# Local attention in half tiles of 58 queries with 64 keys, and the pooled values of the first batch on GpSimd

## The chip, the core and the metric

The kernel runs on one core of a Trainium2 chip. The metric is the device time of one execution in microseconds (us), the median of several runs. Engines are named as in the profile: PE is TensorE's matmuls, PEld its weight loads, DVE is VectorE, ACT is ScalarE, POOL is GpSimd, SP is SyncE, which here only issues DMAs (SPq). L364 is line 364 of the kernel before, unless a line of the changed kernel is named.

## The reference

Attention over 2 batches, 8 heads, 576 tokens and 64 numbers per head is the sum of two paths. One attends from and to means of 4 tokens (144 positions) and repeats the result; the other attends within fewer than 4 tokens. Its output (1152 tokens by 512) goes through a feed-forward network, then through 8 weighted experts.

```python
q_d, k_d, v_d = means of 4 tokens
out_up = np.repeat(softmax(q_d @ k_d.T / 8) @ v_d, 4, axis=2)
mask = np.abs(pos[:, None] - pos[None, :]) < 4
out_local = softmax(np.where(mask, q @ k.T / 8, -1e9)) @ v
x = (out_up + out_local) as (1152, 512)
h = x @ w_in;  x = softplus(h) @ w_out
P = exp(x @ w_gate), rows and columns normalised 8 times
out = sum over e of P[:, e] * (relu(x @ w1[e]) @ w2[e])
```

## The kernel before

Attention is cut into units. A **pooled** unit (`pooled`, 16 of them) is one batch, one half of the 144 means and two heads; a **local** unit (`local`, 20 of them) is one batch, one tile of 116 queries (5 tiles, the last of 112) and four heads. Both have four steps. In a local unit `s1` puts the mask into a PSUM bank with one bf16 matmul (L356), adds the scores of four heads (L364), takes the negative row maximum on DVE (`nm`, L287) and the exponentials on ACT (`e`, L290). `s2` turns the exponentials on PE (L376) and copies them out on ACT (`ptls`, L378). `s3` multiplies by v (L384; a column of ones gives the sums) and scales on DVE (`ull`, L394). `s4` turns the result (L400), adds the pooled path on DVE (`xf`, L406) and leaves x as a rounded and a remainder part on POOL (L419, L420). All matmuls but the mask's are float32: a plain one takes two passes of TensorE, a transpose one, and the trace counts passes (L364 x8 for four matmuls).

The window of a tile of 116 queries is 122 keys (`KW`), and `vw` holds the v rows of that window, loaded by one DMA a tile into a pool of three buffers.

Around the units stand sums for the pooled path: `pool_qk(b, p)` makes `qd` on DVE (L250) and `ks`, `kd` on POOL (L256, L258), and ACT scales `kd` and `k` (L259, L260); `load_vd(b)` adds four v rows (`vs` L277, `vd` L279), on DVE for the first batch and on POOL for the second.

The first weights of the feed-forward network come as float64; `from_double` (L124 to L137) takes them apart: two ACT steps (`cs`, `cm`), then six on DVE, a copy on ACT and a product on POOL (`w`, L137). `prep(n)` does that for the n-th weight tile. The first products of the network are `ph` (L444) and `py` (L486).

The order is written by hand in `run()`. `order` lists the units, `at` says ahead of which unit an extra piece of work is issued (the second batch's loads at 1 and 9, its `pool_qk` at 11 to 14, `prep` at 16, 19, 23 and 29, pieces of the network from 22 on). `emit` lets the four steps of a unit follow two units apart. A scheduler of the tile framework then sets each engine's final order; an engine takes its instructions strictly in that order. `issue_after(i)` keeps what follows behind the instruction i in that order. At most six PSUM banks serve the units. SP issues nearly all DMAs; a DMA also waits for the landing of the one eight places before it.

Of the kernel before, what the change touches and what calls it, by code (L numbers as in the profile page):

```python
# [21 lines left out]
P = 128  # L22
# [4 lines left out]
KW = QT + 2 * (POOLF - 1)  # L27
NQT = -(-S // QT)
NPAIR = H // 2
DA = D + 1  # L30
CH = 384
# [10 lines left out]
WIN = [min(max(QT * t - POOLF + 1, 0), S - KW) for t in range(NQT)]  # L42
OFF = sorted({QT * t - WIN[t] for t in range(NQT)})
# [33 lines left out]
class Net:  # L77
# [11 lines left out]
    def constants(self):  # L89
# [5 lines left out]
        self.mask = self.atp.tile([P, len(OFF), KW], BF16, tag="mask", name="mask", bufs=1)  # L95
        self.maskf = self.convp.tile([P, len(OFF), KW], F32, tag="cm", name="maskf", bufs=1)
# [109 lines left out]
    def attention_pools(self, stack):  # L206
# [3 lines left out]
        self.vwp = stack.enter_context(tc.tile_pool(name="vwp", bufs=3, side="right"))  # L210
# [51 lines left out]

    def load_vw(self, b, t):
        w = self.vwp.tile([P, H, DA], F32, tag="vw", name=f"vw{b}{t}")
        self.nc.sync.dma_start(out=w, in_=self.a["vw"][b, t].rearrange("p (h d) -> p h d", h=H))
        self.vw[b, t] = w

    def load_vd(self, b):
# [3 lines left out]
        for hf in range(2):  # L272
# [3 lines left out]
            e = nc.vector if b == 0 else nc.gpsimd  # L276
# [6 lines left out]
    def softmax_exp(self, ps, n, m, k, tag):  # L283

        nc = self.nc
        nm = self.atp.tile([m, n], F32, tag="nm" + tag, name="nm")
        nc.vector.tensor_reduce(out=nm, in_=ps, op=ALU.max, axis=AX.X, negate=True)  # L287
        e = self.atp.tile([m, n, k], F32, tag="e" + tag, name="e", bufs=3 if tag == "l" else 2)
        for j in range(n):
            nc.scalar.activation(e[:, j], ps[:, j], AF.Exp, bias=nm[:, j : j + 1])  # L290
        return e
# [55 lines left out]
    def local(self, b, t, g):  # L347
        nc, ident = self.nc, self.ident
        st = {}
        w0 = WIN[t]  # L350
        nq = min(QT, S - QT * t)
        mv = OFF.index(QT * t - w0)

        def s1():
            ps = self.psa.tile([P, 512], F32, tag="a", name="pl")[:nq, : 4 * KW].rearrange("p (j k) -> p j k", j=4)
            nc.tensor.matmul(  # L356
                ps,
                lhsT=self.identb[:nq, :nq],
                rhs=self.mask[:nq, mv : mv + 1, :].to_broadcast([nq, 4, KW]),
                start=True,  # L360
                stop=False,
            )
            for j in range(4):
                nc.tensor.matmul(  # L364
                    ps[:, j],
                    lhsT=self.qT[b, j][:, g, QT * t : QT * t + nq],
                    rhs=self.kT[b, j][:, w0 : w0 + KW],
                    start=False,
                    stop=(j == 3),
                )  # L370
            st["e"] = self.softmax_exp(ps, 4, nq, KW, "l")

        def s2():
            ps = self.psa.tile([P, 512], F32, tag="a", name="ptl")[:KW, : 4 * nq].rearrange("p (j q) -> p j q", j=4)
            for j in range(4):
                nc.tensor.transpose(ps[:, j], st["e"][:, j], ident[:nq, :nq])  # L376
            pt = self.atp.tile([KW, 4, nq], F32, tag="ptl", name="ptls")
# [3 lines left out]
        def s3():  # L381
            ps = self.psa.tile([P, 512], F32, tag="a", name="pvl")[:nq, : 4 * DA].rearrange("p (j d) -> p j d", j=4)
            for j in range(4):
                nc.tensor.matmul(  # L384
                    ps[:, j], lhsT=st["pt"][:, j], rhs=self.vw[b, t][:KW, 4 * g + j], start=True, stop=True
                )
            if g == 1 and NQT * b + t + 3 < B * NQT:
                self.load_vw(*divmod(NQT * b + t + 3, NQT))
            rs = self.atp.tile([nq, 4, 1], F32, tag="rsl", name="rsl")
            nc.vector.tensor_scalar(rs, ps[:, :, D:DA], 1e-9, None, ALU.add)  # L390
            rr = self.atp.tile([nq, 4, 1], F32, tag="rrl", name="rrl")
            nc.vector.reciprocal(rr, rs)
            ul = self.atp.tile([nq, 4, D], F32, tag="ull", name="ull")
            nc.vector.tensor_tensor(ul, ps[:, :, 0:D], rr.to_broadcast([nq, 4, D]), ALU.mult)  # L394
            st["ul"] = ul

        def s4():
            ps = self.psa.tile([P, 512], F32, tag="a", name="pxl")[:, : 2 * nq].rearrange("p (j q) -> p j q", j=2)
            for j in range(2):
                nc.tensor.transpose(  # L400
                    ps[:, j], st["ul"][:, 2 * j : 2 * j + 2].rearrange("p j d -> p (j d)"), ident[:nq, :nq]
                )
# [312 lines left out]
    def run(self):  # L715
# [21 lines left out]
        for t in range(3):  # L737
            self.load_vw(0, t)
# [32 lines left out]

        def prep(n, lag):

            with ExitStack() as st:
                for ins in self.ends[-1 - lag]:
# [165 lines left out]
def arrange(i):  # L941
# [10 lines left out]

    va = np.concatenate([va, np.zeros((B, P - KW, H, DA), f)], 1)
    out["vw"] = np.stack([va[:, w : w + P] for w in WIN], 1).reshape(B, NQT, P, H * DA)
# [3 lines left out]
    r, c = np.arange(QT)[:, None], np.arange(KW)[None]  # L958
    m = [np.where(np.abs(r + o - c) < POOLF, f(0), f(-1e9)) for o in OFF]
    m = np.concatenate([np.stack(m, 1), np.zeros((P - QT, len(OFF), KW), f)], 0)  # L960
    out["mask"] = np.ascontiguousarray(m.astype(f))
# [39 lines left out]
```

## Time and profile before

| | us |
|---|---|
| median of 3 runs | 1067.55 (1067.21 to 1068.75) |
| the profiled execution's own time | 1065.39 |
| its span in the profile | 1063.6 |
| PE busy | 1042.9 (98% of the span) |
| DVE busy | 783.1 (74%) |
| ACT busy | 435.4 (41%) |
| POOL busy | 165.8 (16%) |

The profile is of one execution, 1.8 us longer than its span and 2.2 us under the median. The attention units lie in the first 130 us; from there on PE is busy almost without a gap to the end. So the shares of the whole span tell little of this change, and the views below are cut to the first 130 us. A chain row is a piece of the path that ended last; a timeline row is a run of equal instructions with, in brackets, the idle time ahead of it and what ended that.

### The profile page before, as it was taken

To read this page: it belongs to the slowest core of one execution; us is meant where nothing else is said; L and a number is where in the kernel's file an instruction comes from. 1 tells how busy PE (TensorE), PEld (TensorE's weight loads), DVE (VectorE), ACT (ScalarE), POOL (GpSimd) and SP (SyncE) were. 2 spreads that over 40 slices of the span, in tenths; PEclk is the share of its full clock that TensorE was granted. 3 is DMA by queue.
4 is the path that set the end of the run, shared out by engine and by line. 5 is a ranking of instruction groups with operands and counts; after the bars stand their busy time and mean duration, and the time that the engine had idled before them with its cause. 6 is when DMAs were issued, how large, how long until landed. Compare 5 with 4: busy or idle time off the path is not lost.

```text
span 1063.6 us, 16117 instructions
## 1 busy us (share of the span) xinstructions
PE 1042.9 (98%) x6421; PEld 959.9 (90%) x6421; DVE 783.1 (74%) x1466; ACT 435.4 (41%) x815; POOL 165.8 (16%) x218
## 2 busy tenths in 40 slices
PE   7899999999999999999999999999999999999998
PEld 4789999999998899898989989898998989899896
DVE  6698699999997687784947658484765848576572
ACT  4688687766743433241413324141331414133130
POOL 3463300001112220211202011120201112020000
PEclk9899999999999999999999999999999999999999
DMA  9541032222111221111211111121111112110003
GB/s 250 163 153 62 2 120 79 79 80 80 41 40 40 79 80 40 40 41 39 80 40 40 41 40 41 40 80 40 40 40 40 41 40 79 40 41 1 1 2 89
DMA packets 13035, 63.99 MB, mean 60 GB/s; under 512 B 1760, under 2 KB 2016, under 8 KB 6496
## 3 DMA queue, kind: packets, MB, share of 16 engines
q1 hardware_dynamic: 12320, 61.79, 17.8%
q10 hardware_dynamic: 640, 1.18, 0.4%
q8 instruction: 50, 0.82, 0.3%
q14 instruction: 25, 0.20, 0.1%
HBM read 60.60 MB, written 2.36 MB: 59 GB/s over the span
## 4 chain that ended last, share of the span: by engine, by line
PE 87%; DVE 8%; ACT 2%; DMA 2%; POOL 1%; issue 1%; SPq 0%; DVEq 0%; ACTq 0%
PE po L586 37%; PE pu L537 33%; PE ph L444 7%; PE py L486 6%; PE pl L364 1%; DVE h L465 1%; DMA vr<-in_vp 1%; PE pvl L384 1%; DMA k<-in_k 1%; DVE r L461 1%; DVE l L462 1%; PE pvd L325 1%; DVE l L463 1%; DVE yp L498 0%; PE ptl L376 0%
## 5 line engine op out<-in xcount | busy, mean ns | idle before, releaser
L537 PE MATMUL pu<-T,a 128*128 128x320 f32 (+1 forms) x2688 | 354.2, 293 | 1.4 <-DVE yp L498 1.4
L537 PEld LDWEIGHTS pu<-T,a 128*128 128x128 f32 x2688 | 351.4, 188 | 3.0 <-issue 1.6
L608 DVE SCALAR_TENSOR_TENSOR acc<-po,prob,acc 128x512 f32<-128x512 f32 x126 | 94.1, 749 | 173.5 <-PE po L586 173.5
L586 PE MATMUL po<-w,h 128*128 128x512 f32 x960 | 221.3, 390 | 0.0
L586 PEld LDWEIGHTS po<-w,h 128*128 128x128 f32 x960 | 179.9, 188 | 37.3
L188 ACT CAST w<-raw 128x1024 fp32r<-128x1024 f32 x32 | 33.4, 1052 | 271.4 <-PE po L586 271.4
L586 PE MATMUL po<-w,h0a 128*128 128x512 f32 x576 | 142.3, 390 | 0.6 <-DVE w L189 0.6
L157 POOL TENSOR_TENSOR s<-raw 128x256 f32<-128x256 f32 x32 | 28.5, 891 | 677.6 <-DVE a L168 473.0
L586 PEld LDWEIGHTS po<-w,h0a 128*128 128x128 f32 x576 | 107.3, 188 | 22.5 <-DVE w L189 1.0
L486 PE MATMUL py<-h,w 128*128 128x384 f32 x576 | 104.0, 336 | 1.3 <-DVE h L465 0.8
L444 PE MATMUL ph<-x,w 128*128 128x384 f32 x576 | 104.1, 336 | 0.0
L486 PEld LDWEIGHTS py<-h,w 128*128 128x128 f32 x576 | 99.7, 188 | 2.3 <-DVE h L465 1.3
L444 PEld LDWEIGHTS ph<-x,w 128*128 128x128 f32 x576 | 99.8, 188 | 0.0
L549 ACT ACTIVATE h<-c 128x320 fp32r<-128x320 f32 x128 | 58.6, 468 | 79.8 <-DVE c L560 79.8
L550 DVE SCALAR_TENSOR_TENSOR h<-c,h 128x320 fp32r<-128x320 f32 x128 | 68.1, 540 | 0.3
L560 DVE TENSOR_TENSOR c<-v,pu 128x256 f32<-128x256 f32 (+1 forms) x128 | 57.8, 451 | 11.1 <-PE pu L537 8.2
L549 ACT ACTIVATE h0a<-c 128x256 fp32r<-128x256 f32 x96 | 37.5, 417 | 50.7 <-DVE c L560 50.4
L189 DVE TENSOR_TENSOR w<-raw,w 128x1024 fp32r<-128x1024 f32 x32 | 39.0, 1220 | 22.1 <-ACT w L188 22.1
L586 PE MATMUL po<-w,h0b 128*128 128x512 f32 x192 | 54.2, 389 | 0.0
L586 PEld LDWEIGHTS po<-w,h0b 128*128 128x128 f32 x192 | 36.0, 188 | 7.5
L558 ACT COPY p<-pu 128x256 f32<-128x256 f32 (+1 forms) x64 | 25.1, 392 | 36.1 <-PE pu L537 34.5
L550 DVE SCALAR_TENSOR_TENSOR h0a<-c,h0a 128x256 fp32r<-128x256 f32 x96 | 39.1, 420 | 0.8 <-ACT h0a L549 0.3
(141 smaller groups left out, 1243.2 us busy)
## 6 DMA issues: line engine op xcount, KB each, us to landing
raw<-in_w SPq DMA_DIRECT2D x48, 1024.0 KB, 4.9
vw<-in_vw SPq DMA_DIRECT2D x10, 260.0 KB, 2.9
vr<-in_vp SPq DMA_DIRECT2D x4, 640.0 KB, 8.8
k<-in_k SPq DMA_DIRECT2D x8, 288.0 KB, 6.2
out<-acc SPq DMA_DIRECT2D x5, 256.0 KB, 2.0
q<-in_q SPq DMA_DIRECT2D x8, 144.0 KB, 5.9
out<-acc SPq DMA_DIRECT2D x8, 128.0 KB, 2.3
q0a<-in_q ACTq DMA_DIRECT2D x4, 144.0 KB, 5.6
```

The lines of the kernel that those rows point to most:

```text
L157: nc.gpsimd.tensor_tensor(s[:, 0], a21, a22, ALU.add)
L188: nc.scalar.copy(w[:, 0], raw)
L189: nc.vector.tensor_tensor(w[:, 1], raw, split(w[:, 0]), ALU.subtract)
L444: nc.tensor.matmul(ps[:, i], lhsT=wv[:, a, k, fo : fo + P], rhs=x[:, b, k], start=(n == 0), stop=(n == 3 * KD - 1),)
L486: nc.tensor.matmul(ps[:, a], lhsT=w[:, i, d * P : (d + 1) * P], rhs=h[:, j, f], start=(n == 0), stop=(n == 3 * NFT - 1),)
L537: nc.tensor.matmul(ps, lhsT=w[:, x, a, k], rhs=t[:, y, b, k], start=(m == 0), stop=(m == 5))
L549: act = nc.scalar.activation(hi, src, AF.Relu)
L550: dve = nc.vector.scalar_tensor_tensor(lo, src, 0.0, split(hi), ALU.max, ALU.subtract)
L558: nc.scalar.copy(to, ps)
L560: nc.vector.tensor_tensor(to, src, ps, ALU.add)
L586: nc.tensor.matmul(ps, lhsT=self.h[s, i, f][:, at * P : (at + 1) * P], rhs=w[:, j], start=(n == 0), stop=(n == 3 * NFT - 1),)
L608: nc.vector.scalar_tensor_tensor(acc, ps, pe, acc, ALU.mult, ALU.add)
```

## The change

Each local unit now computes two halves of 58 queries, each as 64 rows against its own window of 64 keys. The two halves of a head lie above each other on 128 partitions: the scores are eight float32 matmuls, each into 64 partitions by 64 columns, and the mask is one matmul of 4 x 64 columns in place of 4 x 122. The exponentials of two heads are then turned together, two transposes of 128x128 in place of four. The product with v takes two heads in one matmul: the v rows of two heads stand on the two halves of the partitions beside blocks of zeros (`places_v`, three fixed buffers, the zeros set once by POOL), four matmuls of 130 columns in place of four of 65. The last turn is a plain matmul with columns of the identity, which drops the 6 rows too many of each half, in place of a transpose; in the last tile it is done in two parts. The v window is loaded by two DMAs of 130 KB in place of one of 260 KB.

The pooled v of the first batch (`vs`, `vd`) moves from DVE to POOL. The second batch's `pool_qk` and the first `prep` are kept behind the last softmax that was issued before them (`self.begun`), and the first `prep` is issued at unit 15 in place of 16.

```diff
-KW = QT + 2 * (POOLF - 1)
+HQ = QT // 2
+KW = HQ + 2 * (POOLF - 1)
...
+    def places_v(self):
+        self.vring = [
+            self.vwp.tile([P, 2, 2, NPAIR, DA], F32, tag=f"vw{i}", name=f"vw{i}", bufs=1) for i in range(VR)
+        ]
+        for w in self.vring:
+            for r in range(2):
+                self.nc.gpsimd.memset(w[(1 - r) * D : (2 - r) * D, :, r], 0.0)
+
     def load_vw(self, b, t):
-        w = self.vwp.tile([P, H, DA], F32, tag="vw", name=f"vw{b}{t}")
-        self.nc.sync.dma_start(out=w, in_=self.a["vw"][b, t].rearrange("p (h d) -> p h d", h=H))
+        w = self.vring[(NQT * b + t) % VR]
+        for r in range(2):
+            self.nc.sync.dma_start(out=w[r * D : (r + 1) * D, :, r], in_=self.a["vw"][b, t, r])
...
-            e = nc.vector if b == 0 else nc.gpsimd
+            e = nc.gpsimd
...
-        nc.vector.tensor_reduce(out=nm, in_=ps, op=ALU.max, axis=AX.X, negate=True)
+        dve = nc.vector.tensor_reduce(out=nm, in_=ps, op=ALU.max, axis=AX.X, negate=True)
...
+        self.begun = (dve.ins, act.ins)
...
-            for j in range(4):
-                nc.tensor.matmul(
-                    ps[:, j],
-                    lhsT=self.qT[b, j][:, g, QT * t : QT * t + nq],
-                    rhs=self.kT[b, j][:, w0 : w0 + KW],
+            for u in range(2):
+                n0, w0 = ROW[2 * t + u], WIN[2 * t + u]
+                for j in range(4):
+                    nc.tensor.matmul(
+                        ps[u * KW : (u + 1) * KW, j],
+                        lhsT=self.qT[b, j][:, g, n0 : n0 + KW],
+                        rhs=self.kT[b, j][:, w0 : w0 + KW],
...
-            for j in range(4):
-                nc.tensor.transpose(ps[:, j], st["e"][:, j], ident[:nq, :nq])
+            for j in range(2):
+                nc.tensor.transpose(ps[:, j], st["e"][:, 2 * j : 2 * j + 2].rearrange("p j k -> p (j k)"), ident)
...
-            for j in range(4):
-                nc.tensor.matmul(
-                    ps[:, j], lhsT=st["pt"][:, j], rhs=self.vw[b, t][:KW, 4 * g + j], start=True, stop=True
-                )
+            for u in range(2):
+                for j in range(2):
+                    nc.tensor.matmul(
+                        ps[u * D : (u + 1) * D, 2 * j : 2 * j + 2],
+                        lhsT=st["pt"][:, j, u * D : (u + 1) * D],
+                        rhs=self.vw[b, t][:, u, :, 2 * g + j],
...
+                if last == KW:
+                    cols = ident.rearrange("p (u q) -> p u q", u=2)[:, :, :HQ]
+                    nc.tensor.matmul(ps[:, j], lhsT=ul, rhs=cols, start=True, stop=True)
+                    continue
+                for o, n, c in ((0, HQ, 0), (HQ, nq - HQ, last)):
+                    nc.tensor.matmul(ps[:, j, o : o + n], lhsT=ul, rhs=ident[:, c : c + n], start=True, stop=True)
...
+        def second(p):
+            with ExitStack() as st:
+                for ins in self.begun:
+                    st.enter_context(self.tc.issue_after(ins))
+                self.pool_qk(1, p)
...
-                for ins in self.ends[-1 - lag]:
+                for ins in self.begun if n == 0 else self.ends[-1 - lag]:
...
-            at.setdefault(11 + p, []).append(lambda p=p: self.pool_qk(1, p))
-        for n, lag, u in zip(range(2 * NFT), (1, 1, 0, 0), (16, 19, 23, 29)):
+            at.setdefault(11 + p, []).append(lambda p=p: second(p))
+        for n, lag, u in zip(range(2 * NFT), (1, 1, 0, 0), (15, 19, 23, 29)):
```

On POOL the work of the start stands as follows, first before, from the zeros of the second batch's q on (`ks02` is the pair of first sums for batch 0, pair 2 of the keys; `vs10` the first half of batch 1's v):

```order
L228 MEMSET q10_211 64x576 x2
...
L258 TENSOR_TENSOR kd03_165<-ks03_163 128x144
L256 TENSOR_TENSOR ks10_560<-k1_210 128x288
L256 TENSOR_TENSOR ks11_599<-k1_210 128x288
L258 TENSOR_TENSOR kd10_562<-ks10_560 128x144
L258 TENSOR_TENSOR kd11_601<-ks11_599 128x144
L256 TENSOR_TENSOR ks12_647<-k1_210 128x288
L256 TENSOR_TENSOR ks13_691<-k1_210 128x288
L277 TENSOR_TENSOR vs10_471<-vr10_469 72x1024
L277 TENSOR_TENSOR vs11_476<-vr11_474 72x1024
L279 TENSOR_TENSOR vd1_467<-vs10_471 72x8x64
```

In the changed kernel the same place reads:

```order
L274 MEMSET vw0_192 64x2x260 x2
...
L291 TENSOR_TENSOR vs01_188<-vr01_186 72x1024
L293 TENSOR_TENSOR vd0_179<-vs00_183 72x8x64
L262 TENSOR_TENSOR kd03_165<-ks03_163 128x144
L260 TENSOR_TENSOR ks10_579<-k1_219 128x288
L293 TENSOR_TENSOR vd0_179<-vs01_188 72x8x64
L260 TENSOR_TENSOR ks11_618<-k1_219 128x288
L291 TENSOR_TENSOR vs10_488<-vr10_486 72x1024
L291 TENSOR_TENSOR vs11_493<-vr11_491 72x1024
L293 TENSOR_TENSOR vd1_484<-vs10_488 72x8x64
L262 TENSOR_TENSOR kd10_581<-ks10_579 128x144
```

Six zero fills and the first batch's `vs` and `vd` have come in, and `kd10`, which stood ahead of the second batch's `vs` and `vd`, now stands behind three of these four.

On ACT, at the place where the second batch begins, the order before is this (`cm_776` and `cs_778` take apart the first float64 weights, `raw0`):

```order
L378 COPY ptls_533<-ptl_528 122x464
L290 ACTIVATE e_523<-pl_515,nm_521 116x122 x4
L318 COPY ptds_579<-ptd_574 72x288
L343 COPY upT0_191<-pxd_592 128x72
L126 ACTIVATE cm_776<-raw0_480 128x1024
L124 ACTIVATE cs_778<-raw0_480 128x1024
L290 ACTIVATE e_571<-pd_566,nm_569 72x144 x2
L259 ACTIVATE kd12_649<-kd12_649 128x144
L378 COPY ptls_623<-ptl_618 122x464
```

And in the changed kernel:

```order
L394 COPY ptls_552<-ptl_549 128x256
L304 ACTIVATE e_544<-pl_532,nm_542 128x64 x4
L263 ACTIVATE kd10_581<-kd10_581 128x144
L264 ACTIVATE k1_219<-k1_219 128x576
L333 COPY ptds_598<-ptd_593 72x288
L304 ACTIVATE e_590<-pd_585,nm_588 72x144 x2
L358 COPY upT0_191<-pxd_611 128x72
L263 ACTIVATE kd11_620<-kd11_620 128x144
L264 ACTIVATE k1_219<-k1_219 128x576
L394 COPY ptls_644<-ptl_641 128x256
```

The two instructions on `raw0` have gone from here (they now follow 15 rows behind `e_590`), and the scaling of `kd10`, which stood 16 rows ahead of `cm_776` before, now comes in their neighbourhood, ahead of `ptds_598` and `e_590`.

On PE one local unit's scores and what follows them (of several units, since the steps overlap) read before:

```order
L356 MATMUL pl_605<-mask_173,identb_171 116x488
L364 MATMUL pl_605<-k0_121,q0a_115 116x122
L364 MATMUL pl_605<-k1_125,q0a_115 116x122
L364 MATMUL pl_605<-k2_145,q0b_116 116x122
L364 MATMUL pl_605<-k3_157,q0b_116 116x122
L376 MATMUL ptl_618<-ident_169,e_523 122x116 x4
L384 MATMUL pvl_625<-vw01_194,ptls_533 116x65 x4
L400 MATMUL pxl_636<-ident_169,ull_546 128x116 x2
```

And in the changed kernel, the eight scores in their order:

```order
L370 MATMUL pl_624<-mask_173,identb_171 128x256
L380 MATMUL pl_624<-k0_121,q0a_115 64x64
...
L380 MATMUL pl_624<-k3_157,q0b_116 64x64
L380 MATMUL pl_624<-k0_121,q0a_115 64x64
...
L380 MATMUL pl_624<-k3_157,q0b_116 64x64
L392 MATMUL ptl_641<-ident_169,e_544 128x128 x2
L401 MATMUL pvl_646<-vw1_193,ptls_552 64x130 x4
L425 MATMUL pxl_657<-ident_169,ull_565 128x116 x2
```

The steps keep their order; the number of matmuls and their shapes change, and scores and v products now fill 64 of TensorE's 128 columns of outputs at a time.

## Rows read from the trace of the kernel before

**Rows 1.** windows of 10 us: busy us (x instructions) of each engine, clock, DMA share, GB/s

```profile
40.00:50.00 10.00, 6.03 (x34) 5.70 (x35) 4.97 (x14) 6.19 (x17) 3.95 (x7) 0.67 0.35 144
...
60.00:70.00 10.00, 8.70 (x85) 8.07 (x84) 9.22 (x29) 7.41 (x17) 8.18 (x9) 1.00 0.38 135
...
90.00:100.00 10.00, 9.80 (x84) 9.37 (x82) 10.00 (x24) 7.89 (x23) 5.36 (x3) 1.00 0.39 133
```

**Rows 2.** PE timeline, 20 to 75 us: start, us, what, idle ahead and its releaser

```profile
21.27 0.71 PE L301 MATMUL pd<-kd,qd 128*72 128x144 f32 x4 [3.37 <-DVE qd L250]
...
40.20 0.42 PE L400 MATMUL pxl<-ident,ull 116*128 116x116 f32 x2 [0.59 <-DVE ull L394]
44.39 0.56 PE L356 MATMUL pl<-mask,identb 116*116 116x488 bf16 x1 [3.77 <-ACT e L290]
...
72.82 1.12 PE L444 MATMUL ph<-x,w 128*128 128x384 f32 x5
```

**Rows 3.** ACT timeline, 29 to 43 us

```profile
29.99 0.69 ACT L260 ACTIVATE k<-k 128x576 f32<-128x576 f32 x1
...
36.91 0.40 ACT L318 COPY ptds<-ptd 72x288 f32<-72x288 f32 x1 [0.21 <-PE ptd L316]
...
41.64 1.13 ACT L126 ACTIVATE cm<-raw 128x1024 f32<-128x1024 f32 x1 [3.99 <-DMA raw<-in_w]
```

**Rows 4.** chain of waits around the long wait and behind it: start, us, what

```profile
39.65 1.26 POOL vd L279
...
42.68 1.12 ACT cs L124
...
44.95 1.63 PE pl L364 x8
...
54.31 1.13 DVE cs L134
```

**Rows 5.** chain of waits, the parts of a local unit and one pooled product

```profile
24.18 0.51 PE pvd L325 x8
...
29.46 0.21 PE pl L356
29.67 0.83 PE pl L364 x8
...
30.90 0.77 PE pvl L384 x8
...
35.87 0.21 PE pxl L400 x2
...
38.44 0.40 PE ptl L376 x4
```

**Rows 6.** PE timeline around a product from one partition in the gate

```profile
349.21 1.07 PE L586 MATMUL po<-w,h 128*128 128x512 f32 x4
350.20 0.38 PE L678 MATMUL pgb<-gm,ones 1*128 1x1 f32 x2
350.51 0.98 PE L586 MATMUL po<-w,h 128*128 128x512 f32 x3
```

**Rows 7.** POOL timeline, 0 to 75 us

```profile
1.06 4.96 POOL L228 MEMSET q<- 64x576 f32 x8
...
33.79 4.67 POOL L277 TENSOR_TENSOR vs<-vr 72x1024 f32<-72x1024 f32 x2 [3.21 <-DVE rrd L335]
...
40.87 0.42 POOL L258 TENSOR_TENSOR kd<-ks 128x144 f32<-128x144 f32 x1
...
66.08 2.36 POOL L137 TENSOR_TENSOR w<-cs,ch 128x1024 fp32r<-128x1024 f32 x1
```

**Rows 8.** DVE timeline, the second half of the first batch's v

```profile
18.73 1.22 DVE L277 TENSOR_TENSOR vs<-vr 72x1024 f32<-72x1024 f32 x1 [1.93 <-DMA vr<-in_vp]
```

**Rows 9.** costs by form, first 220 us: busy us, mean ns, idle ahead and its releaser

```profile
L287 DVE TENSOR_REDUCE nm<-pl 116x4 f32<-116x488 f32 x16 | 10.5, 657 | 5.3 <-PE pl L364 5.1
...
L130 DVE SCALAR_TENSOR_TENSOR ch<-raw,cm 128x1024 int32<-128x1024 int32 x12 | 15.0, 1246 | 0.1
```

More of the change, by code (lines that the diff above doesn't have):

```diff
@@ L30 @@
 DA = D + 1
+VR = 3
 CH = 384
@@ L41 @@
 ITERS = 8
-WIN = [min(max(QT * t - POOLF + 1, 0), S - KW) for t in range(NQT)]
-OFF = sorted({QT * t - WIN[t] for t in range(NQT)})
+WIN = [min(max(HQ * t - POOLF + 1, 0), S - KW) for t in range(2 * NQT)]
+ROW = [min(HQ * t, S - KW) for t in range(2 * NQT)]
+OFF = [tuple(ROW[t] - WIN[t] for t in (2 * u, 2 * u + 1)) for u in range(NQT)]
+KINDS = sorted(set(OFF))
 NRING = 6
@@ L94, in constants @@
         nc.vector.tensor_copy(self.identb, self.ident)
-        self.mask = self.atp.tile([P, len(OFF), KW], BF16, tag="mask", name="mask", bufs=1)
-        self.maskf = self.convp.tile([P, len(OFF), KW], F32, tag="cm", name="maskf", bufs=1)
+        self.mask = self.atp.tile([P, len(KINDS), KW], BF16, tag="mask", name="mask", bufs=1)
+        self.maskf = self.convp.tile([P, len(KINDS), KW], F32, tag="cm", name="maskf", bufs=1)
         nc.sync.dma_start(out=self.maskf, in_=self.a["mask"])
@@ L381, in s3 @@
         def s3():
-            ps = self.psa.tile([P, 512], F32, tag="a", name="pvl")[:nq, : 4 * DA].rearrange("p (j d) -> p j d", j=4)
-            for j in range(4):
-                nc.tensor.matmul(
-                    ps[:, j], lhsT=st["pt"][:, j], rhs=self.vw[b, t][:KW, 4 * g + j], start=True, stop=True
[L386 to L389, printed above, removed]
+            ps = self.psa.tile([P, 512], F32, tag="a", name="pvl")[:, : 4 * DA].rearrange("p (j d) -> p j d", j=4)
@@ new lines, in s3 @@
+            for u in range(2):
[4 more added lines that the diff above has]
+                        rhs=self.vw[b, t][:, u, :, 2 * g + j],
+                        start=True,
+                        stop=True,
+                    )
+            if g == 1 and NQT * b + t + VR < B * NQT:
+                self.load_vw(*divmod(NQT * b + t + VR, NQT))
@@ L390, in s3 @@
+            rs = self.atp.tile([P, 4, 1], F32, tag="rsl", name="rsl")
             nc.vector.tensor_scalar(rs, ps[:, :, D:DA], 1e-9, None, ALU.add)
-            rr = self.atp.tile([nq, 4, 1], F32, tag="rrl", name="rrl")
+            rr = self.atp.tile([P, 4, 1], F32, tag="rrl", name="rrl")
             nc.vector.reciprocal(rr, rs)
-            ul = self.atp.tile([nq, 4, D], F32, tag="ull", name="ull")
-            nc.vector.tensor_tensor(ul, ps[:, :, 0:D], rr.to_broadcast([nq, 4, D]), ALU.mult)
+            ul = self.atp.tile([P, 4, D], F32, tag="ull", name="ull")
@@ L736, in run @@
         self.load_vd(0)
-        for t in range(3):
+        self.places_v()
+        for t in range(VR):
             self.load_vw(0, t)
@@ L951, in arrange @@
     va[..., :D] = vt
-    va = np.concatenate([va, np.zeros((B, P - KW, H, DA), f)], 1)
-    out["vw"] = np.stack([va[:, w : w + P] for w in WIN], 1).reshape(B, NQT, P, H * DA)
+    vw = np.stack([va[:, w : w + KW] for w in WIN], 1).reshape(B, NQT, 2, KW, NPAIR, 2, DA)
+    out["vw"] = np.ascontiguousarray(vw.transpose(0, 1, 5, 3, 2, 4, 6))
     vp = np.ascontiguousarray(vt).reshape(B, 2, GH, POOLF * DM)
@@ L957, in arrange @@
     out["ident"] = np.eye(P, dtype=f)
[L958 to L961, printed above, removed]
+    r, c = np.arange(KW)[:, None], np.arange(KW)[None]
+    m = [[np.where(np.abs(r + o - c) < POOLF, f(0), f(-1e9)) for o in k] for k in KINDS]
+    out["mask"] = np.ascontiguousarray(np.stack([np.concatenate(x) for x in m], 1).astype(f))
     out["wg"] = np.ascontiguousarray(i["moe2_w_gate"].reshape(KD, P, E).transpose(1, 0, 2))
```

33 lines of the change are left out of this document (17 added, 16 removed).

## The prediction

> **What bounds the kernel now.** I read the table of 10 us windows first. PE is full nearly everywhere from 75 us on (9.80 of 10 even where DVE is at 10.00), and the two windows with room are 40 to 50 us (PE 6.03, granted clock 0.67) and 60 to 70 us (PE 8.70) [rows 1]. So work added to PE behind 40 us costs its own length, and work taken from DVE, ACT or POOL pays only where PE waits for it. The timeline of PE comes second: its long waits are 3.37 us ahead of 21.27 and 3.77 us ahead of 44.39 [rows 2]. The second is traced in ACT's timeline: ACT stands 3.99 us in front of `cm`, for the weights `raw` that land at 41.6 [rows 3], then runs `cm` and `cs`, and only then the exponentials that free PE. In the chain of waits this shows as POOL's `vd` at 39.65 (whose engine was on the same stretch), ACT's `cs` at 42.68, and then eight passes of scores that take 1.63 us [rows 4] where they take 0.83 elsewhere [rows 5]: TensorE is at 1.2 GHz after that wait and at 2.4 GHz elsewhere. A mean clock of 0.67 over 10 us is 6.6 us at half speed, 3.3 us of PE work lost.
>
> **PE's work in a local unit.** Before, in the chain's steps: mask 0.21, scores 0.83, turns 0.40, v product 0.77, last turn 0.21, together 2.42 us [rows 5]. After: the mask has 256 columns in place of 488, 0.21 x 256/488 = 0.11. The scores are eight float32 matmuls, 16 passes of 64 columns. The nearest row is the pooled v product, 65 columns, 0.51/8 = 0.064 a pass [rows 5], so 16 x 0.063 = 1.00; the bounds are the present pass of 122 columns scaled by columns (0.104 x 64/122 = 0.054, so 0.87) and not scaled at all (16 x 0.104 = 1.66). The two turns of 128 columns cost 0.11 each, 0.22. The v product has four matmuls, eight passes of 130 columns, 8 x 0.104 x 130/122 = 0.89. The last turn is now a plain matmul, four passes of 116 columns in place of two, 0.42. Sum 2.64, or +0.22 a unit; bounds +0.09 and +0.88. The four units of the last tile have eight passes of 58 and 54 columns, at 0.064 each 0.51 against 0.42: +0.4 in all. About eight of the 20 units lie ahead of the long wait, where more PE work only shortens an idle PE; twelve lie behind it: 12 x 0.22 + 0.4 = +3.0 us (bounds +1.5 and +11).
>
> The scores and the v product put their output in 64 partitions, the mask and both turns in 128, so PE changes the shape of its tile four times a unit. No row of before has that change. The nearest is the gate's product from one partition between products from 128: its two passes stand between po's runs of four and three, and from 349.21 to 351.49 these nine passes take 2.28 us [rows 6]. Seven of po cost at most 7 x 1.07/4 = 1.87 and two small ones some 0.06 each as in [rows 5]; 0.29 is left, say 0.30 for going in and out. The opposite bound is zero, and below zero if the halves run side by side. I take zero, since here the partitions of the operands stay 128 and only the outputs are halved; that choice decides more than any other, and the 0.30 is a rival below.
>
> **The start.** POOL gets six zero fills of 520 numbers a row ahead of the others: 4.96/8 x 520/576 x 6 = 3.4 us [rows 7], so its first key sums go from 6.0 to 9.4. The first batch's v sums leave DVE (two of 1.22 us for `vs`, the second at 18.73, released by its DMA [rows 8], and two shorter ones) and cost 4.67/2 = 2.33 each on POOL [rows 7]. The second half lands at 18.7, so `vs01` ends at 21.1, and behind it the order has `vd0` (1.26), `kd03` (0.42), `ks10` (twice the columns of a `kd`, some 0.7) and the last `vd0` (1.26 as the `vd` of [rows 4]): 24.7. The first pooled v product, now at 24.18 [rows 5], then comes at least 0.5 us late. I cost this at nothing: PE stands still later for something POOL does only once batch 1's v has landed. If that cover goes, it is +0.5. Doing it on POOL also leaves PE's dummy products and the clock there as they are: it was 3.37 us idle ahead of 21.27 and the four passes after it took 0.71, a full-speed time [rows 2].
>
> **The long wait.** ACT no longer meets the weights' `cm` there; it meets the scaling of `kd10`, tied behind the last softmax. `kd10` is on POOL behind `vs10`, `vs11` and one `vd1`: 33.79 + 4.67 [rows 7] + 1.26 [rows 4] + 0.42 [rows 7] = 40.1. Queued behind it on ACT are the key scaling of 0.69, `ptds` of 0.40 [rows 3], and the exponentials; PE's next turn waits for that `ptds`. With a kd of about 0.3 that is 41.5. PE comes to that turn at 38.44 now [rows 5] and, with the start and two or three longer units, at about 38.8 then, so it is idle 2.7 us in place of 3.77. Then come turn 0.22, v product 0.89, last turn 0.42 and the wait for `ull` as before, 0.59 [rows 2]: the mask of the next unit starts at 43.6, against 44.39: -0.7. An idle of 3.37 kept the clock, the one of 3.77 did not, so with 2.7 I expect it kept: -3.3.
>
> **The float64 weights.** `cs` and `cm` come some 9 us later on ACT (three local units and a pooled one stand ahead of them now, 3 x 2.64 and about 1 by PE's pace), so six DVE steps (the longest 1.25 [rows 9]) fall between 52 and 60 us, where DVE is the chain; in before the latter half of them stood there too, as with `cs` at 54.31 [rows 4]. Each unit's maximum (0.657 for 488 columns [rows 9]) shrinks to about 0.4, which gives back 0.24 x 7 = 1.7 there. What is left lies between 0 and +2.9. I take +0.4, near the lower end, because the product of the weights is needed only with x, and x comes sooner: the second weight's product of 2.36 [rows 7] stood ahead of the last casts of x and now stands behind them, so the run of `ph` now at 72.82 [rows 2] can start some 2.4 us earlier. That lead is not an extra gain: what PE does from there on is the same work, and it holds only the idle time already counted. ACT's lighter exponentials and copies gain nothing, as ACT is not waited for outside the long wait.
>
> **Sum.** -0.7 (wait) - 3.3 (clock) + 3.0 (PE work) + 0.4 (DVE) = -0.6 us, against the profiled execution: 1065.4 to 1064.8. That execution lies 2.2 under the median, so on the median 1067.55 - 0.6 = 1066.9.
>
> **Rivals.**
> First, faster: the halves share the array. Scores of the second half could start beside the last pass of the first, and so with v: 0.063 + 0.111 = 0.17 a unit, twelve times -2.0; and the lighter DVE takes away PE's idle 1.3 us of 60 to 70 us [rows 1]. -0.6 - 2.0 - 1.3 = -3.9, 1063.6. For it speaks that each half has its own columns; against it that now a pass never overlaps the next by more than the trace's equal spacing shows. The Trainium skill, "TensorEngine Tiling (Array Packing)", section on the tiling modes' key properties, says that different tiles can load weights and multiply in parallel; no run of before shows it.
>
> Second, slower: each change of the tile's shape costs what the gate's does, 0.30 us for in and out [rows 6]. There are two such trips a local unit and some three more where other work is put between: 43, of which 16 fall ahead of the long wait and are hidden. 27 x 0.30 = 8.1; -0.6 + 8.1 = +7.5, 1075.0. It decides from 0.10 us a trip on (2.7 us, then the kernel is at 1069.6). For it: the gate's rows; against: there the partitions of the operands change, here only those of the output. The same page of the Trainium skill, "TensorEngine Tiling (Array Packing)", states in the same section that a change of the tiling mode drains TensorE; the gate's row agrees with it, and no row of before has it for halved outputs.
>
> Third, slower, the change does not do what it says: the long wait stays. Three more v-window DMAs at the start are in the queue ahead of batch 1's v, and each DMA waits for the eighth before it. If its landing slips 1.5 us, `kd10` slips with it, PE's idle is past 3.77 again (it is from 1.1 us on), the clock falls (+3.3) and the lead of 0.7 goes: -0.6 + 4.0 = +3.4, 1071.0.
>
> **Chances.** My forecast 0.45, with a range of its own of 1064.6 to 1069.1; the halves side by side 0.25; the price of the tile's change 0.18; the wait stays 0.12. A difference of 0.2%, 2.1 us, is about what a measurement of this kernel can tell from none. Of my forecast's 0.45, 0.11 is faster than that, 0.29 within, 0.05 slower; with the rivals: faster 0.11 + 0.25 = 0.36, same 0.29, slower 0.05 + 0.18 + 0.12 = 0.35. The range goes from 1062.0 (the halves overlapping somewhat more than in my working) to 1075.5 (the full price of the tile's change).
>
> **What would show it.** Right: in the chain of the changed kernel a local unit takes about 2.6 us on PE, with eight passes of the first half's scores at 0.5; the wait ahead of the turn at about 41.5 is 2 to 3 us and is released by ACT, behind POOL's `kd`; the scores after it take no more than elsewhere; the clock of 40 to 50 us is over 0.9; the first long run of `ph` starts before 72. Wrong: a gap or a long pass at each change between mask, scores, turn and v product; passes of 64 columns at 0.10; a clock under 0.8 in 40 to 50 us; or PE idle between 52 and 66 us by more than the 1.3 us that it has now in 60 to 70, which would say that the weights' DVE steps came too late.

## The result and the profile after

The changed kernel takes 1074.2 us (median of 6, 1073.0 to 1075.8) beside 1066.9 for the kernel before (median of 6): ratio 1.0071, 95% interval 1.0054 to 1.0088. It is slower by some 7.5 us; 1066.9 was forecast. The profiled execution took 1074.36, its span is 1072.6 and its mean granted clock 0.992, against 0.997 before. The two profiled spans lie 9.0 us apart, somewhat more than the medians.

Where the time goes is read from one mark, the 48th matmul of `py`, behind which both kernels do the same work: before it starts at 128.8 us, after at 137.1, +8.3. It is the last of these twelve passes, before and after:

```profile
126.77 2.35 PE L486 MATMUL py<-h,w 128*128 128x384 f32 x12
```

```profile
135.06 2.34 PE L513 MATMUL py<-h,w 128*128 128x384 f32 x12
```

Three sums up to that mark tell the kinds of loss apart, from the windows of 10 us: idle is 10 less PE's busy time; clock loss is (1 less the granted clock) times 10; the rest is work, among it the dummy products (`pz`, products of zeros that nobody reads). Idle time at half clock is counted in both, so the sums are good to a microsecond or two.

| to the 48th `py` | mark | idle | clock loss | rest |
|---|---|---|---|---|
| before | 128.8 | 13.5 | 3.5 | 111.8 |
| after | 137.1 | 13.2 | 8.6 | 115.3 |
| difference | +8.3 | -0.3 | +5.1 | +3.5 |

The windows of the changed kernel that answer to [rows 1], and the two with the early loss (same columns: PE, PEld, DVE, ACT, POOL busy, clock, DMA, GB/s):

```profile
20.00:30.00 10.00, 7.20 (x64) 6.37 (x59) 3.32 (x11) 3.81 (x14) 4.65 (x6) 0.71 1.07 281
30.00:40.00 10.00, 10.00 (x90) 8.59 (x88) 3.90 (x15) 5.07 (x20) 5.82 (x3) 0.60 0.66 172
40.00:50.00 10.00, 8.77 (x112) 7.25 (x111) 9.25 (x22) 7.39 (x27) 6.12 (x12) 1.00 0.45 164
...
80.00:90.00 10.00, 8.04 (x70) 6.80 (x69) 8.24 (x21) 7.51 (x21) 4.27 (x3) 0.83 0.24 96
```

The window of 40 to 50, at 0.67 before, is now at 1.00: the half speed there has gone, as forecast, and of the long wait for ACT nothing is left, where 2.7 us were forecast. But TensorE is at half speed earlier, from 24 to 38 us, and again from about 86 to 89. The timeline of PE shows what came ahead of both (in brackets: idle time and what ended it); it answers to [rows 2]:

```profile
12.95 2.54 PE L208 MATMUL pz<-z 128*128 128x512 bf16 x11
18.20 0.47 PE L316 MATMUL pd<-kd,qd 128*72 128x144 f32 x2 [2.71 <-ACT kd L263]
...
22.51 0.71 PE L316 MATMUL pd<-kd,qd 128*72 128x144 f32 x4 [2.09 <-ACT kd L263]
23.93 0.32 PE L331 MATMUL ptd<-ident,e 72*72 72x72 f32 x2 [0.71 <-ACT e L304]
24.09 0.29 PE L340 MATMUL pvd<-vd,ptds 72*72 72x65 f32 x2
24.21 1.13 PE L316 MATMUL pd<-kd,qd 128*72 128x144 f32 x4
...
46.18 0.67 PE L425 MATMUL pxl<-ident,ull 128*128 128x116 f32 x4 [1.23 <-DVE rsl L411]
46.69 0.27 PE L370 MATMUL pl<-mask,identb 128*128 128x256 bf16 x1
...
82.46 0.71 PE L316 MATMUL pd<-kd,qd 128*72 128x144 f32 x4 [0.59 <-ACT e L304]
84.54 0.44 PE L331 MATMUL ptd<-ident,e 72*72 72x72 f32 x4 [1.37 <-DVE uld L352]
...
85.36 3.90 PE L471 MATMUL ph<-x,w 128*128 128x384 f32 x12
...
118.82 2.35 PE L471 MATMUL ph<-x,w 128*128 128x384 f32 x12
```

PE waits for `kd` twice and once for `e`, and at 24.21 four passes that took 0.71 at 22.51 take 1.13: the clock has fallen from 2.4 to 1.2 GHz. In the new order all dummies but two stand ahead of 15.5 us, and none between these waits. Before, the wait of 3.37 was followed by seven of them:

```profile
21.82 1.68 PE L204 MATMUL pz<-z 128*128 128x512 bf16 x7
```

The mask that I forecast for 43.6 comes at 46.69. At 85.36 twelve passes of `ph` take 3.90, where they take 2.35 at 118.82.

One local unit at full clock, from 115 us, each step's cost being the distance to the next start; it answers to [rows 5]:

```profile
115.14 0.23 PE L357 MATMUL pxd<-ident,uld 72*128 72x72 f32 x1
115.21 0.28 PE L370 MATMUL pl<-mask,identb 128*128 128x256 bf16 x1
115.42 0.97 PE L380 MATMUL pl<-k,q 128*64 128x64 f32 x16
116.31 0.44 PE L392 MATMUL ptl<-ident,e 128*128 128x128 f32 x2
116.68 0.67 PE L401 MATMUL pvl<-vw,ptls 128*64 128x130 f32 x8
117.28 0.70 PE L425 MATMUL pxl<-ident,ull 128*128 128x116 f32 x4
117.82 0.38 PE L392 MATMUL ptl<-ident,e 128*128 128x128 f32 x2
```

Mask 0.21, scores 0.89, turns 0.37, v product 0.60, last turn 0.54: 2.61, against 2.42 before and 2.64 in the forecast. That the sum fits is luck: two effects that I had as rivals both hold and nearly cancel. The halves share the array: the v product's eight passes of 130 columns take 0.60 where 0.89 was worked out. It is also seen in a unit whose two q tiles have different names (q0a of the second half runs beside q0b of the first):

```profile
57.55 0.45 PE L380 MATMUL pl<-k,q0a 128*64 128x64 f32 x4
57.84 0.22 PE L380 MATMUL pl<-k,q0b 128*64 128x64 f32 x1
57.84 0.27 PE L380 MATMUL pl<-k,q0a 128*64 128x64 f32 x1
```

And every change between 64 and 128 output partitions leaves a pause, which the experiments price. It is contained in the steps next to the change: the mask, with half the columns, still takes 0.21 to the first score.

### The profile page after: what moved, and what is told of

Same layout as the page of the kernel before. It is cut to its first block, busy times and chain, and to the rows that moved or that the text cites. A ratio compares the mean times of both kernels' runs of the same rounds, so it can differ in the third digit from the quotient of the medians.

```text
span 1072.6 us, 16487 instructions
## 1 busy us (share of the span) xinstructions
PE 1051.9 (98%) x6597; PEld 957.7 (89%) x6597; DVE 782.5 (73%) x1462; ACT 429.5 (40%) x815; POOL 179.6 (17%) x228
## 4 chain that ended last, share of the span: by engine, by line
PE 83%; DVE 6%; ACT 1%; issue 0%; DVEq 0%
PE po L613 37%; PE pu L564 32%; PE ph L471 6%; PE py L513 6%; DVE h L492 1%; DVE r L488 1%; DVE l L489 1%; DVE yp L525 0%; DVE l L490 0%; DVE T L554 0%; PE pxl L425 0%; PE pl L380 0%; PE pvl L401 0%; DVE cs L138 0%; DVE a L172 0%
```

## The experiments

Each kernel was timed beside the kernel before on the same chip; its ratio to it is given with its interval, to be read against the changed kernel's 1.0071. The first four pull apart work and clock. In what was expected, theory C is that the clock's early fall costs the time, theory S that each change of the tile's shape does.

**First batch's v sums back on VectorE**

```diff
-            e = nc.gpsimd
+            e = nc.vector if b == 0 else nc.gpsimd
```

> The changed kernel with the first batch's v sums back on VectorE. Theory C (clock): the changed kernel lost time because TensorE idled at 15 to 22 us behind GpSimd's v sums and then ran at 1.2 GHz from 24 to 38 us; with the sums back on VectorE the granted clock of 20 to 40 us should be 1.00 in place of 0.71 and 0.60, the mask at 46.69 us should start at about 43.6, and the whole should take 3 us less than the 1074.2 of the changed kernel, some 1071. Rival S (all of the loss is TensorE's own work in the local units, the early half speed lies under waits): the clock may rise, but the time stays at 1073 to 1075.

Ratio 1.0067 (1.0042 to 1.0091): no gain. The clock did not hold either; TensorE is busy 4.53 of 10 us in 10 to 20 and falls there (clock 0.90, then 0.59 in 20 to 30). With the zero fills still ahead of the key sums, the v sums alone don't decide whether TensorE stands idle, so the run does not separate the theories. Its other three executions, with mean clocks of 0.994 to 0.996, still took 1071.5 to 1072.6, so here the clock alone is not the whole loss.

**One trip a unit**

```diff
-                for k, u in enumerate(live[::STEP]):
+                now = list(enumerate(live[::STEP]))
+                for k, u in now[:1] + now[2:3] + now[1:2] + now[3:]:
```

> The changed kernel with the steps of the units issued in the order scores, v product, turn, last turn, so that scores and v product (outputs of 64 partitions) stand together and TensorE changes its tile's shape twice a local unit in place of four times. Theory S: a change costs about 0.15 us (0.30 for out and back, as the gate's rows gave); one trip less for 20 units, 12 to 16 of them where TensorE sets the end: 3.6 to 4.8 us less than the changed kernel, 1069.5 to 1070.5, and the starts of scores and v product follow each other without the extra 0.09 to 0.15. Rival (64-column passes are slow by themselves, no cost of a change): no difference in the passes' starts, 1074 give or take 1, apart from what the other order does to waits.

Ratio 1.0046 (1.0029 to 1.0064), some 2.7 us less than the changed kernel, though the two intervals overlap. The profiled execution's clock was lower still (0.52 and 0.50 from 20 to 40 us). Its PE timeline:

```profile
114.23 0.27 PE L370 MATMUL pl<-mask,identb 128*128 128x256 bf16 x1
114.43 0.79 PE L380 MATMUL pl<-k,q 128*64 128x64 f32 x13
115.01 0.33 PE L401 MATMUL pvl<-vw,ptls 128*64 128x130 f32 x1
...
115.77 0.44 PE L392 MATMUL ptl<-ident,e 128*128 128x128 f32 x2
116.05 0.60 PE L425 MATMUL pxl<-ident,ull 128*128 128x116 f32 x4
116.58 0.67 PE L401 MATMUL pvl<-vw,ptls 128*64 128x130 f32 x8
```

The v product starts while the last scores run, with no pause, and the unit takes 116.58 - 114.23 = 2.35 in place of 2.61. In the rows theory S holds: 0.26 for one trip saved.

**The kernel before with its mask in two halves**

```diff
-            nc.tensor.matmul(
-                ps,
-                lhsT=self.identb[:nq, :nq],
...
+            for lo, hi in ((0, 64), (64, nq)):
+                nc.tensor.matmul(
+                    ps[lo:hi],
+                    lhsT=self.identb[:nq, lo:hi],
```

> The kernel before with each local unit's mask done as two matmuls of 64 and 52 output partitions, nothing else changed: one trip into and out of the 64-partition tile shape a unit, and nothing that is packed better. Theory S: the two halves of the mask start within 0.02 us of each other and cost 0.2 together as now, with about 0.10 to 0.15 of pause ahead of them and behind them: +0.3 a unit, 20 units, of which 12 to 20 count: +3.6 to +6 us, 1070.5 to 1073. Rival without a cost of the change: side by side +0, one after the other +0.2 a unit, and no pause at either end.

Ratio 1.0070 (1.0047 to 1.0092), 7 us for nothing but this. PE timeline:

```profile
110.00 0.23 PE L342 MATMUL pxd<-ident,uld 72*128 72x72 f32 x1
110.16 0.39 PE L357 MATMUL pl<-mask,identb 116*64 116x488 bf16 x2
110.48 1.09 PE L365 MATMUL pl<-k,q 128*116 128x122 f32 x8
111.41 0.56 PE L377 MATMUL ptl<-ident,e 116*122 116x116 f32 x4
```

The two masks together take 0.32 where one took 0.21, and both are done 0.39 after the first starts, where one takes 0.37 by itself, so they run side by side; the pause shows ahead of them (0.16 where 115.14 to 115.21 above has 0.07), behind them (+0.11) and in the scores (0.93 against 0.83): 0.09 + 0.11 + 0.10 = 0.30 a trip, as was estimated from the gate [rows 6]. So the price of a trip, a rival in the forecast, is measured by itself: 20 x 0.30 = 6.0 of the 7. In the profiled execution the rest up to the 48th `py` rises by 5.4 and the clock loss by 1.6.

**Last turn by transposes against a permuted identity**

```diff
+        self.perm = self.atp.tile([P, 2, P], F32, tag="perm", name="perm", bufs=1)
...
-                    nc.tensor.matmul(ps[:, j], lhsT=ul, rhs=cols, start=True, stop=True)
...
+                nc.tensor.transpose(ps[:, j], ul, self.perm[:, int(last != KW)])
```

> The changed kernel with its last turn as two transposes of 128x128 against a column-permuted identity (made once on VectorE, seven small copies) in place of plain float32 matmuls. The last turn then takes two passes of 0.11 us in place of four, and in the last tile in place of eight: -0.22 for 16 units and -0.66 for 4, -6.2 us in all, of which the part behind 40 us counts, 12 units: about -4.4, some 1069.8. If the plain turn isn't on the path that sets the end (waits for VectorE rule that stretch), the time stays within 1 us of 1074.

Ratio 1.0054 (1.0034 to 1.0074): 1.8 us less, not 4.4, and the two intervals overlap. The turn itself does what was expected:

```profile
114.21 0.28 PE L378 MATMUL pl<-mask,identb 128*128 128x256 bf16 x1
...
116.28 0.44 PE L431 MATMUL pxl<-perm,ull 128*128 128x128 f32 x2
116.56 0.38 PE L400 MATMUL ptl<-ident,e 128*128 128x128 f32 x2
```

It is 0.28 against 0.54, a unit takes 116.56 - 114.21 = 2.35, and in the sums to the 48th `py` the rest falls by 6.9 (108.4). But idle rises to 14.9 and clock loss to 10.3, with falls at 80 to 90, as in the changed kernel, and at 100 to 110 (0.83 each). In this execution the gain of work was handed back in part; that a lighter PE meets VectorE's waits sooner, and so loses clock, is the likely reason, but no run shows it by itself.

The next runs take up the clock.

**Seven more dummies**

```diff
-                nc.tensor.matmul(
+                mm = nc.tensor.matmul(
...
+            if (b, hf, p) == (0, 0, 3):
+                with self.tc.issue_after(mm.ins):
+                    self.warm(7)
```

> The changed kernel with seven more dummy products on TensorE behind the pooled scores at 22.5 us, where the kernel before has seven and the changed one none. Theory C (the early fall of the clock costs time): granted clock 1.00 in 20 to 40 us in place of 0.71 and 0.60, TensorE then idles for GpSimd's kd as predicted (mask now at 46.69 then at about 44), 2 to 3 us less: a ratio to before of 1.0045 to 1.0055 against the changed kernel's 1.0071. Rival: what the clock gives, the later waits take back: ratio 1.006 to 1.008 with the clock at 1.00.

Ratio 1.0093 (1.0075 to 1.0112), the wrong way. The edit also moved the older dummies in the scheduler's order: PE was busy only 2.20 us in 10 to 20, behind a wait of 4.76 and ahead of one of 6.98, and the clock fell there (0.55). It did not make the condition it was meant to make and says nothing for or against.

**The start as before**

```diff
-        for w in self.vring:
-            for r in range(2):
-                self.nc.gpsimd.memset(w[(1 - r) * D : (2 - r) * D, :, r], 0.0)
...
-        for r in range(2):
-            self.nc.sync.dma_start(out=w[r * D : (r + 1) * D, :, r], in_=self.a["vw"][b, t, r])
+        self.nc.sync.dma_start(
+            out=w, in_=self.a["vw"][b, t].rearrange("p (u r j d) -> p u r j d", u=2, r=2, j=NPAIR)
+        )
...
-            e = nc.gpsimd
+            e = nc.vector if b == 0 else nc.gpsimd
...
```

> The changed kernel with the start as before: the first batch's v sums on VectorE, and the v window loaded with its blocks of zeros by one DMA of 260 KB, so no zero fills on GpSimd and three window loads at the start. Theory C: no half speed in 10 to 40 us, no long wait at 40 (kd of the second batch is scaled early); the mask now at 46.69 us comes at 41 to 43; what is left of the loss is TensorE's own +0.19 a unit and the stall at 82 to 89: ratio 1.003 to 1.005. Rival (the work of the units alone): ratio stays at 1.006 to 1.008.

Ratio 1.0022 (1.0007 to 1.0037): two thirds of the loss are gone, with the local units as in the changed kernel. Its windows:

```profile
20.00:30.00 10.00, 8.74 (x104) 7.33 (x106) 6.85 (x21) 5.88 (x23) 2.80 (x5) 1.00 1.06 313
30.00:40.00 10.00, 8.77 (x107) 7.19 (x107) 8.59 (x24) 8.28 (x30) 4.97 (x5) 1.00 0.85 197
```

Full clock, no long wait; the mark stands at 130.1, with an idle of 11.0, a clock loss of 1.8 and a rest of 117.3. Against the kernel before that is -2.5, -1.7 and +5.5: the wait and the clock that the forecast counted on are gained here, and the work of the units takes them back and more. The rows of the units give 20 x 0.19 and some 0.26 more for each of the four in the last tile, 4.8; the +3.5 of the changed kernel and the +5.5 here lie on either side, as near as such sums come.

**Third weight's product on VectorE**

```diff
-        e = nc.gpsimd if n < NFT else nc.vector
+        e = nc.gpsimd if n < NFT and n != 2 else nc.vector
```

> The changed kernel with the product of the third float64 weight tile on VectorE in place of GpSimd. Theory L: at 81.98 us VectorE's l takes 2.30 us in place of 0.55 because GpSimd's product (2.96 us, normally 2.36) runs beside it; TensorE then waits 1.37 us for uld and runs at 1.2 GHz to 89. With the product on VectorE (1.22 us by its row) both are gone: the clock of 80 to 90 us is 1.00, 1.5 to 3 us less, ratio 1.0045 to 1.0057. Rival (TensorE waits there for VectorE's amount of work, whoever runs beside it): the wait stays above 1 us, the ratio at 1.007.

The mechanism is there, the gain is not. In the changed kernel VectorE's `l` is stretched beside GpSimd's product (first fence VectorE, second GpSimd):

```profile
81.98 2.30 DVE L489 TENSOR_TENSOR l<-l,r 128x384 f32<-128x384 f32 x1
```

```profile
80.91 2.96 POOL L141 TENSOR_TENSOR w<-cs,ch 128x1024 fp32r<-128x1024 f32 x1 [4.18 <-DVE rsd L348]
```

The product does not stretch all that runs beside it: VectorE's `r` at 81.12 keeps its 0.54. With the product on VectorE the same `l` takes 0.55:

```profile
86.08 0.55 DVE L489 TENSOR_TENSOR l<-l,r 128x384 f32<-128x384 f32 x1
```

PE's wait for `uld` is gone and the clock of 80 to 90 us is 1.00. Yet the ratio is 1.0085 (1.0058 to 1.0113): its clock at 20 to 40 us was 0.51 and 0.50, worse than in the changed kernel, and the 48th `py` came at 137.7. What the second fall costs can't be read beside a deeper first one.

**All three mended**: the start as before, one trip a unit and the permuted last turn, by the edits above together.

> The changed kernel with three edits together: the start as before (window with zeros in one DMA, v sums on VectorE), one trip of the tile's shape a unit (scores and v product together), last turn by two transposes against a permuted identity. TensorE's work falls by about 6 + 6 us, under that of the kernel before (2.61 - 0.30 - 0.22 = 2.1 a unit against 2.42). Theory S and C together: as fast as before or faster, ratio 0.996 to 1.001. Rival (VectorE's work between 50 and 105 us sets the end and a lighter TensorE only idles, so that its clock falls more often): ratio 1.002 to 1.006, with more than 15 us of TensorE idle in the first 140.

1060.0 us, ratio 0.9949 (0.9934 to 0.9964): faster than both kernels, 0.5% under the one before. Mark at 122.3, clock loss 1.7, rest 106.7, idle 13.9. From the mask to the next unit's v product it is 2.13:

```profile
103.26 0.27 PE L376 MATMUL pl<-mask,identb 128*128 128x256 bf16 x1
...
105.39 0.67 PE L407 MATMUL pvl<-vw,ptls 128*64 128x130 f32 x8
```

The last four split the start and check the ties.

**Zeros from memory, v sums on GpSimd**: the edit of the start without its two lines on `e`.

> The changed kernel with only the v window's zeros moved into the loaded data (one DMA of 260 KB a tile in place of two of 130 KB, no zero fills on GpSimd); the first batch's v sums stay on GpSimd. Beside the changed kernel (ratio 1.0071), the same with v sums on VectorE (1.0067) and both together (1.0022) this fills the fourth corner. Theory F (the fills and the extra DMAs are the loss at the start): ratio 1.002 to 1.0035, clock 1.00 in 20 to 40 us. Rival V (either of the two is enough for TensorE to stand idle and fall to 1.2 GHz): ratio 1.005 to 1.008, clock under 0.9 somewhere between 15 and 40 us.

Ratio 1.0037 (1.0019 to 1.0055), between the two. Its six executions had mean clocks from 0.992 (1073.1 us, the profiled one, 0.67 and 0.65 from 20 to 40 us) to 1.000 (1066.7). With the sums on GpSimd, or with the fills and the second DMA a tile (0.990 to 0.996 in the first run above), the mean clock varied from execution to execution; without both it was 0.995 to 0.998 in all ten of the kernel with the start as before. Dummies alone don't keep it: in the profiled execution six of them stand between 18 us and a wait of 2.45 and two behind it, and at 23.4 the clock falls all the same. Whether the fills and the DMAs are undone ahead of the sums or after them, they carry the larger part of the loss at the start: 0.0034 or 0.0045 of the 0.0049, each good to some 0.002.

**The ties undone**, on the kernel with the start as before:

```diff
-                for ins in self.begun if n == 0 else self.ends[-1 - lag]:
+                for ins in self.ends[-1 - lag]:
...
-            at.setdefault(11 + p, []).append(lambda p=p: second(p))
-        for n, lag, u in zip(range(2 * NFT), (1, 1, 0, 0), (15, 19, 23, 29)):
+            at.setdefault(11 + p, []).append(lambda p=p: self.pool_qk(1, p))
+        for n, lag, u in zip(range(2 * NFT), (1, 1, 0, 0), (16, 19, 23, 29)):
```

> The changed kernel with the start as before (ratio 1.0022) and with the order around it as before too: second batch's key sums and first float64 weights not tied behind the last softmax, the first weights at unit 16. If the ties are worth something: ACT stands in front of the weights again near 40 us, TensorE idles 2 to 4 us there and may fall to 1.2 GHz: ratio 1.0035 to 1.006. If they are worth nothing: within 0.001 of 1.0022.

Ratio 1.0015 (1.0001 to 1.0029), the same as 1.0022: the ties are worth nothing that can be told. The long wait stays away without them too (PE's longest between 26 and 50 us is 0.63), and the clock holds:

```profile
40.00:50.00 10.00, 9.46 (x123) 7.71 (x122) 7.86 (x26) 7.97 (x27) 7.73 (x11) 1.00 0.68 259
```

So it does not take the ties to remove it.

**Zero fills added to the kernel before**

```diff
+        zeros = self.atp.tile([P, 6, 130], F32, tag="zf", name="zf", bufs=1)
+        for i in range(6):
+            self.nc.gpsimd.memset(zeros[(i % 2) * D : (i % 2 + 1) * D].rearrange("p a b -> p (a b)")[:, : 520], 0.0)
```

> The kernel before with six zero fills of 64 x 520 on GpSimd added at the start (3.3 us, into a buffer that nobody reads), nothing else. Theory F: the key sums that feed TensorE come 2 to 3 us later, TensorE idles and then runs at 1.2 GHz for some us between 12 and 40: ratio 1.002 to 1.005. Rival (the DMAs of the window, not the fills, do it; a late start is taken up by the wait at 40 us): ratio 0.999 to 1.001.

Ratio 0.9993 (0.9979 to 1.0007). Theory F falls in its simple form: 3.3 us of GpSimd's time at the start cost nothing that can be told. In the profiled execution the clock does fall early (0.87 in 10 to 20, 0.95 in 20 to 30), but the fall at 40 to 50 is shorter (0.83 for 0.67), and the clock loss up to the mark is 3.5 as before. The scheduler put four of the fills ahead of the first key sums and two behind them, a lighter case than the changed kernel's six. The second DMA of each tile was not tried by itself.

**The combined kernel with two trips**: all of it but the regrouped steps.

> The combined kernel (ratio 0.9949) without its regrouped steps: start as before, last turn by two transposes, but four changes of the tile's shape a unit again. Theory S: 0.30 us more a unit, 12 to 20 units: +3.6 to +6 us, ratio 0.9983 to 1.0005. Rival (TensorE had slack there): ratio 0.995 to 0.997.

Ratio 1.0017 (0.9995 to 1.0038), but the ten executions fall into two groups by their clock. Four with a mean granted clock of 0.995 to 0.998 took 1063.4 to 1064.7; six with 0.988 to 0.990 took 1069.2 to 1070.9: same program, 6 us. The profiled one is of the second group, with early windows as in the changed kernel:

```profile
20.00:30.00 10.00, 7.48 (x53) 6.19 (x54) 5.67 (x14) 3.53 (x12) 1.33 (x2) 0.67 1.05 310
30.00:40.00 10.00, 10.00 (x92) 8.73 (x91) 4.24 (x17) 4.96 (x20) 4.45 (x5) 0.65 0.62 151
...
80.00:90.00 10.00, 8.69 (x51) 7.03 (x51) 5.55 (x14) 7.29 (x22) 3.48 (x2) 0.57 0.22 93
```

It falls a second time, in 80 to 90, so the 6 us are the price of both falls. The dummies do not keep the clock here either: ten stand ahead of a wait of 2.77 and three behind it, and ahead of 24 us it falls. At equal clocks the regrouping is worth 1064 - 1060 = 4 us, 0.30 for 13 of the 20 units. In the changed kernel all six executions have 0.989 to 0.992.

## Why the prediction was wrong

- **The long wait (-0.7) and the clock behind it (-3.3).** The wait went and 40 to 50 us ran at full clock. The mask still came 3.1 us later than forecast, because PE arrived late: the clock had fallen before. The reason that I gave, ACT's order behind the ties, is not shown to be the one: the wait is gone without the ties as well, and what removes it there stays open.
- **The start, "I cost this at nothing".** This is the step that failed. I looked for the cover of a delay in GpSimd's chain and found it, and wrote that the dummy products and the clock would stay as they are, from one wait of 3.37 us that had not cost the clock. In its place the runs showed half speed from 24 to 38 us, a clock loss of 8.6 in all where 0.2 was forecast (3.5 less 3.3). With the start as before it is 1.8 and the ratio 1.0022: about 5 of the 7.5 us. My sign, full-speed passes behind a wait, is also a weak one: the passes at 22.51 had it, and the clock fell 1.7 us later. I did not read in the new order that the dummies would stand ahead of 15.5 us, with waits of 2.71, 2.09 and 0.71 behind; that their place is what costs the clock is a guess, since it fell in two runs with dummies around the waits.
- **The work of a unit (+0.22).** Measured +0.19, out of wrong terms: the v product 0.60 for 0.89 and the scores 0.89 for 1.00 (halves side by side, in the scores only in part), against the mask 0.21 for 0.11, the turns 0.37 for 0.22 and the last turn 0.54 for 0.42 (each with pauses of the tile's change in it). In the last tile the last turn takes 0.80 (131.27 to 132.07) for 0.51: passes of 58 columns took 0.10, where I had 0.064.

```profile
131.27 0.99 PE L428 MATMUL pxl<-ident,ull 128*128 128x58 f32 x8
132.07 0.42 PE L471 MATMUL ph<-x,w 128*128 128x384 f32 x1
```

- **No price for a change of the tile's shape.** I took zero; it is 0.30 for out and back. The rule of the Trainium skill, "TensorEngine Tiling (Array Packing)", on its tiling modes' key properties, that a change of the mode drains TensorE, agrees with the rows of the split mask; the other rule there, that tiles work in parallel, agrees with the rows of q0a beside q0b. Each was a rival, with 0.18 and 0.25; that both could hold was not among my cases. The pauses, two trips in each unit, are in the measured +0.19 already, and against the forecast the halves pay for them. The second rival's 1075.0 is near the time, but by a sum that lacks the halves' gain and the clock's loss.
- **Eight units hidden ahead of the wait.** There was no wait left in front of which PE could be idle, so nearly all of the added work counted: +3.5 in the rest, and +5.5 in the kernel with the start as before, where +3.0 was forecast for the twelve units behind the wait. This is the second step that failed, and most of what is left at 1.0022.
- **The float64 weights (+0.4).** The first long run of `ph` started at 71.2, ahead of 72.82 as forecast. Beyond it, at 82 to 89 us, PE waited for VectorE, held up by GpSimd's product, and lost clock: a loss that no step of mine had. The same fall stands in the kernel with the start as before (0.91 in 70 to 80 and in 80 to 90), as its only clock loss, 1.8. Whether it costs anything by itself stays open, since in the run without it the early fall was deeper.

What sets the clock's fall in a given execution is not settled, nor which part of the new start costs most. The last kernel above, whose start is that of the one at 1.0022 but for seven small copies on VectorE, had a mean clock of 0.990 or less in six executions of ten; the combined kernel, with the same copies, held 0.996 to 0.998 in all four.

## What to carry to other kernels

When a change delays the first work of TensorE, follow the new order of its dummy products and waits, not only the engine that got longer: here the new start cost about 5 us, mostly as half speed, and one kernel's executions lay 6 us apart by whether the clock fell. Look at the clock of several executions before a profile of one is taken for the kernel. Matmuls with 64 output partitions pay when they stand together, 0.30 us being the price of going there and back: with one trip less and the turn by transposes a unit took 2.13, against 2.61 in the changed kernel and 2.42 before. A plain float32 matmul is a dear way to pick columns: against a permuted identity a transpose does it in half the passes.

## What the hardware showed that I had not expected

- Float32 matmuls into the two halves of the output partitions run side by side: a unit's eight v passes of 130 columns take 0.60 us, pauses included, where eight of 65 columns took 0.77.
- With about 60 moving columns, the price of a float32 pass goes with the size of its weights: 0.10 us with 128 columns of weights and 58 moving (0.80 for eight), 0.096 with 116 and 65 (the v product before, 0.77 for eight), 0.064 with 72 and 65 (the pooled one, 0.51 for eight [rows 5]).
- A GpSimd product of 128x1024 beside VectorE stretched one VectorE instruction from 0.55 to 2.30 us and left another, of the same shape, at 0.54.
- Twelve passes of `ph` behind a wait of 1.37 us took 3.90 in place of 2.35 us: TensorE fell to 1.2 GHz here with no longer wait than 1.37 just ahead of it, and another of 0.59 two microseconds before. At the start of the kernel before, a wait of 3.37 did not cost the clock.
